# Routing attention and a hard-swish feed-forward: the first division a double step sooner, and two short settings instead of three behind each indexed transfer

## The chip, the core and the metric

The kernel runs on one core of a Trainium2 chip. The core has five engines, each with an instruction stream of its own: TensorE (PE in the profile; its weight loads are PEld), VectorE (DVE), ScalarE (ACT), GpSimd (POOL) and SyncE (SP). SyncE issues most of the transfers; ScalarE issues some, and GpSimd issues the indexed ones. Each engine takes its instructions in the order in which the kernel wrote them, and waits on semaphores where it needs another engine's result or a transfer's landing.

The metric is the device time of one execution in microseconds. The kernel before takes 937.38 us (median of three runs, from 936.87 to 940.17).

## What is computed

Attention with routing: queries and keys are assigned to the nearest of 16 centroids of their head, and a query sees only keys of its own cluster. The output, with the heads put side by side, goes through a feed-forward block with the hard-swish gate.

```python
B, H, S, D = 4, 8, 768, 64                       # 16 centroids per head
q_assign = argmax(q_n @ c_n, -1); k_assign = argmax(k_n @ c_n, -1)
scores = where(q_assign[:, None] == k_assign[None, :], q @ k.T / sqrt(D), -1e9)
attn = softmax(scores)
x = (attn @ v).transpose(0, 2, 1, 3).reshape(B * S, H * D)      # 3072 x 512
h = x @ w_in                                     # 512 x 2048
g = h * clip(h + 3, 0, 6) / 6
out = g @ w_out                                  # 2048 x 512
```

The matrices w_in and w_out arrive as 64-bit floats and are turned into 32-bit floats on the chip, by integer operations on their two halves.

## The kernel before

**Pairs of heads.** The 32 heads go through in 16 pairs, two heads to 128 partitions. Four pairs make up one batch (NKT = 4). The first eight pairs (batches 0 and 1) are done in full: all 768 x 768 scores of a head are computed, a mask made from the cluster assignment is added by a second matmul, and ScalarE takes the exponentials. The last eight pairs (batches 2 and 3) are sorted by cluster, so that only bands of the score matrix are needed.

**The early part** is a loop over double steps (`for n in range(0, ..., 2)`, L1399). One pair takes twelve steps (six double steps): two halves of the queries (hf) by six blocks of keys (j). A double step does the scores (L407) and exponentials (L430) of steps n and n + 1, adds the exponentials up on GpSimd (L437, L440) for the sums of the softmax, and multiplies the exponentials of the two steps before with the values (L450). In between stand the preparation of the next pair (transposes L325, cluster scores L344, `route` L351 to L378, `route_turn` L380 to L391), the loads of the q, k and v of coming pairs (in the double step with r == 6, by `load`, L209), and a handful of steps that decode the weights (`decoding_steps`, L224 to L270). One chunk of the weights takes five such steps, and its first also issues the load of the chunk two further on (L222, tile `raw`).

**Sums and division.** When both halves of a pair have been added up, `sum_up` (L467) lets TensorE add over the partitions (pd, L476), ScalarE copies the result (dn, L480), and SyncE stores it in device memory (sums, L483). The attention output without division (num, L459) is stored as xd by a transfer that stands in a list (L461). After the last pair of a batch `load_sums` (L487) reads all the sums of the batch back in another layout (plain, L489), `invert` takes their reciprocal on VectorE (L492) and stores it (rd, L493), and `complete` appends the three blocks of 256 tokens of the batch to `waiting` and calls `load_block` (L550). That one loads a block of xd (xb, L556) and the reciprocals for it, spread over the partitions (rb, L560). `divide` (L507) then multiplies xb by rb on VectorE (L510), in place. The feed-forward matmuls read xb.

**The order of these stages** is made by two lists. Whatever is put into `later` in one double step moves to `checks` at the end of that double step, and is executed at the end of the next one, by `check_all` (L1362). In batch 0 each stage puts the next into `later`, so that read-back, reciprocal, block load and division stand one double step apart. In batch 0 the sums of the last pair (pair 3) are stored in the double step n = 50, the read-back is issued at the end of n = 52, the reciprocal at the end of n = 54 (behind the `route` of the next pair), the block load at the end of n = 56 and the division at the end of n = 58. The first feed-forward matmuls (ph, L634) come in the double step n = 60, the first entry of `up_at` (L1343). In batch 1 the read-back is put out the same way, in the last double steps of the loop, while its `invert` and `complete` have fixed places in the late part (points 2 and 4, L1445).

**The late part** (L1443) is a plan of points. Each point issues what `late_plan` lists for the late pairs and then one item of the feed-forward of the batches that are ready. One pair starts every 28 points (SLOT). The feed-forward works on blocks of 256 tokens as 2 x 2 blocks with seven products instead of eight; for each of its units it loads sums of weight blocks (tx, L573, issued by ScalarE) from device memory.

**Indexed transfers.** For each late pair GpSimd scatters the rows of q (`scatter` with a = 0: qd, L1094) and of k and v together (a = 1: kvd, L1094) to their ranks, twelve transfers each (two heads by six columns of 128 rows), and later gathers the rows of the output back (`gather`: xn, L1109), twelve more. Behind each of these 36 transfers per pair stands `pause()`, which issues PAUSE settings of the one-column tile w_low (L1086). They write the value that is in it already.

Of the kernel before, what the change touches and what calls it, by code (L numbers as in the profile page):

```python
# [122 lines left out]
def fast_path(ctx, tc, ok, q, k, v, centroids, moe_w_in, moe_w_out, out):  # L123
# [57 lines left out]
    later = []  # L181

    def scratch(shape, name, dtype=F32):

        if st["early"]:
            return psum_m.tile(shape, dtype, name=name, tag="m")
        return psum_t.tile(shape, dtype, name=name, tag="t")
# [279 lines left out]
    def sum_up(g):  # L467
        b, kt = divmod(g, NKT)
        if kt == 0:
            for name in ("sums", "rd"):  # L470
                st[name, b] = dram.tile([NKT, 2, S], F32, name=f"{name}{b}")
        pd = scratch([P, 512], "pd")[:, 0:HALF]
        for t in range(2):
            for hf in range(2):
                r = (2 * t + hf) * 2 * C
                nc.tensor.matmul(  # L476
                    pd[r : r + 2 * C], lhsT=ones[:, 0 : 2 * C], rhs=st["acc", g, hf][:, t], start=True, stop=True
                )
        dn = nump.tile([P, HALF], F32, name="dn")
        nc.scalar.copy(out=dn, in_=pd)  # L480
        for hf in range(2):
            st.pop(("acc", g, hf))
        nc.sync.dma_start(st["sums", b][kt].rearrange("t (hf c) -> (t hf) c", hf=2), dn[0 : P : 2 * C])  # L483
        if kt == NKT - 1:
            later.append(lambda: load_sums(b))

    def load_sums(b):  # L487
        tok = plain[:, b]
        nc.sync.dma_start(tok, st["sums", b].rearrange("k t s -> (k t s)").rearrange("(p n) -> p n", p=P))  # L489

        def invert():
            nc.vector.reciprocal(out=tok, in_=tok)  # L492
            nc.sync.dma_start(st["rd", b].rearrange("k t s -> (k t s)").rearrange("(p n) -> p n", p=P), tok)  # L493
            return complete

        def complete():
            waiting.extend((b, m) for m in range(NHC))
            load_block()
            if b == 0:
                later.append(lambda: divide(0, 0))  # L500

        if b == 0:
            later.append(lambda: later.append(invert()))
        else:
            st["invert"], st["complete"] = invert, complete

    def divide(b, m):  # L507
        if ("rb", b, m) in st:
            xb, rb = st["xb", b, m], st.pop(("rb", b, m))
            nc.vector.tensor_tensor(out=xb, in0=xb, in1=rb, op=ALU.mult)  # L510
# [39 lines left out]
    def load_block():  # L550
        if waiting and st["free"]:
            b, m = waiting.pop(0)
            st["free"] = False
            xb = st["xb", b, m] = xbp.tile([P, NKT, 2 * P], F32, name="xb")
            part = slice(2 * m * P, 2 * (m + 1) * P)
            nc.sync.dma_start(xb, st["xd", b][:, :, part])  # L556
            if ("rd", b) in st:
                rb = st["rb", b, m] = xbp.tile([P, NKT, 2 * P], F32, name="rb", tag="xs")
                for t in range(2):
                    nc.sync.dma_start(  # L560
                        rb[t * D : (t + 1) * D], st["rd", b][:, t, part].unsqueeze(0).to_broadcast([D, NKT, 2 * P])
                    )
# [516 lines left out]
            op0=ALU.min, op1=ALU.max,  # L1079
        )  # L1080

    PAUSE = 3

    def pause():
        for _ in range(PAUSE):
            nc.gpsimd.memset(w_low, W_LOW)  # L1086
# [287 lines left out]
    with tc.manual_schedule():  # L1374
# [24 lines left out]
        for n in range(0, total + lag_d + 2, 2):  # L1399
# [11 lines left out]
            if m >= 0 and m % per_pair == per_pair - 1:  # L1411
                sum_up(m // per_pair)
                ready(m)
# [355 lines left out]
@with_exitstack  # L1769
def kernel(  # L1770
    ctx: ExitStack,
    tc: tile.TileContext,
    q: bass.AP,
    k: bass.AP,
    v: bass.AP,
    centroids: bass.AP,
    moe_w_in: bass.AP,
    moe_w_out: bass.AP,
    out: bass.AP,
):  # L1780
    ins = (q, k, v, centroids, moe_w_in, moe_w_out)
    flagp = ctx.enter_context(tc.tile_pool(name="flagp", bufs=1))
    ok = flagp.tile([1, 1], I32, name="ok")
    with ExitStack() as inner:
        good = fast_path(inner, tc, ok, *ins, out)
    with tc.If(good == 0):
        with ExitStack() as inner:
            general_path(inner, tc, *ins, out)
# [32 lines left out]
```

## Time and profile before

| | |
|---|---|
| median of three runs | 937.38 us (936.87 to 940.17) |
| the profiled execution | 940.63 us, of which the span of the program's instructions is 938.7 us |
| TensorE busy | 920.1 us (98%) |
| GpSimd busy | 586.9 us (63%), 1313 instructions |
| VectorE busy | 552.8 us (59%) |
| ScalarE busy | 334.7 us (36%) |
| transfers | 124.77 MB, 133 GB/s on average |

In a row of the timeline stand the start and the length in us, the engine (with a q where its sequencer issues a transfer), the line of the kernel, the operation, what it writes and reads, how many such instructions are merged in the row, and in brackets how long the engine idled before and what ended that. In a row of the groups stand, after the bar, the busy time in us, the mean of one in ns, and after the second bar the idle time before them with its causes. In a row of the waits stand the waiting engine, line and tile, what was waited for, the total in us, how often, and the longest. In a row of the windows stand the stretch, its length, then the busy time and number of instructions of PE, PEld, DVE, ACT and POOL, the granted clock of TensorE, the share of the transfer engines, and GB/s. In the chain stand start, length and what held the chain.

### The profile page before, as it was taken

The numbers are of one execution on the slowest core, as the hardware profiler recorded it, in microseconds if no ns is written. First come the engines' busy times: TensorE is split into PE (matmuls) and PEld (weight loads), VectorE is DVE, ScalarE is ACT, GpSimd is POOL, SyncE is SP. The second block draws the span as 40 slices with busy tenths as digits, with TensorE's granted clock in tenths as the row PEclk, the third lists the DMA queues.
The fourth block names the chain that finished last, engine by engine and source line by source line (L and its number), as shares of the span: only waits on it lengthen the run. The fifth ranks groups of instructions, "written<-read, shape, count | busy, mean of one in ns | idle before, by whom it ended". The sixth has DMA issues, their size and how long they took to land.

```text
span 938.7 us, 17537 instructions
## 1 busy us (share of the span) xinstructions
PE 920.1 (98%) x6350; PEld 721.7 (77%) x6350; DVE 552.8 (59%) x1299; ACT 334.7 (36%) x667; POOL 586.9 (63%) x1313
## 2 busy tenths in 40 slices
PE   8999989999999999999999999999999999999997
PEld 5444445555898898797897978888888899999996
DVE  6667647778876385384483573563571555536261
ACT  6888767765012332222232241241322311212020
POOL 3877876779376787878778777777887060303030
PEclk9999999999999999999999999999999999999999
DMA  8444565450465566474772835645563334323120
GB/s 199 137 134 128 160 181 141 140 166 34 119 196 164 140 173 154 131 208 93 197 199 80 218 101 155 167 146 131 132 175 96 87 84 120 100 73 108 57 68 27
DMA packets 177024, 124.77 MB, mean 133 GB/s; under 512 B 135681, under 2 KB 155169, under 8 KB 176929
## 3 DMA queue, kind: packets, MB, share of 16 engines
q1 hardware_dynamic: 153968, 76.52, 31.1%
q10 hardware_dynamic: 13744, 34.44, 12.5%
q0 software_dynamic: 9216, 12.60, 4.4%
q8 instruction: 52, 0.85, 0.4%
q14 instruction: 44, 0.35, 0.1%
HBM read 95.11 MB, written 28.41 MB: 132 GB/s over the span
## 4 chain that ended last, share of the span: by engine, by line
PE 91%; DVE 3%; ACT 2%; DMA 2%; issue 1%; SPq 0%; DVEq 0%; ACTq 0%
PE Y L725 18%; PE uY L686 16%; PE X L725 13%; PE uX L686 12%; PE ps L407 7%; PE pv L450 6%; PE ph L634 3%; PE pv L1196 3%; PE ps L978 2%; PE ps L1139 2%; PE pcs L344 1%; PE pv L1139 1%; PE pqk L325 1%; DMA rb<-rd 1%; PE pd L476 1%
## 5 line engine op out<-in xcount | busy, mean ns | idle before, releaser
L440 POOL TENSOR_TENSOR acc<-acc,ex 128x768 f32<-128x768 f32 x64 | 124.8, 1950 | 29.9 <-ACT ex L430 26.5
L1094 POOL DMA_INDIRECT qd<-qn,pos x96 | 98.7, 1028 | 45.7 <-DVE tx L576 17.9
L1109 POOL DMA_INDIRECT xn<-xsd,pos x96 | 92.3, 961 | 49.5 <-ACT sx L517 27.9
L676 POOL TENSOR_TENSOR g_sb<-g_sb 128x256 f32<-128x256 f32 x52 | 39.2, 776 | 121.7 <-DVE g_sb L520 120.6
L517 ACT ACTIVATE sx<-g_sb,half_c 128x512 f32<-128x512 f32 x88 | 63.6, 723 | 144.1 <-DVE g_sb L697 111.4
L1086 POOL MEMSET w_low<- 128x1 f32 x864 | 91.6, 106 | 33.4
L1094 POOL DMA_INDIRECT kvd<-kvn,pos x96 | 97.3, 1013 | 21.7 <-issue 21.7
L732 DVE TENSOR_TENSOR y<-y,Y 128x256 f32<-128x256 f32 x47 | 19.8, 421 | 128.4 <-PE Y L725 100.1
L686 PE MATMUL uX<-xb,w_in_sb 128*128 128x128 f32 x704 | 93.0, 275 | 0.0
L725 PE MATMUL X<-w_out_sb,g_sb 128*128 128x256 f32 x384 | 90.3, 382 | 0.0
L725 PE MATMUL Y<-T,g_sb 128*128 128x256 f32 x384 | 88.0, 381 | 0.0
L725 PE MATMUL Y<-w_out_sb,g_sb 128*128 128x256 f32 x384 | 87.7, 380 | 0.0
L686 PEld LDWEIGHTS uX<-xb,w_in_sb 128*128 128x128 f32 x704 | 85.7, 192 | 0.0
L725 PEld LDWEIGHTS Y<-T,g_sb 128*128 128x128 f32 x384 | 72.1, 190 | 13.0 <-issue 3.3
L725 PEld LDWEIGHTS X<-w_out_sb,g_sb 128*128 128x128 f32 x384 | 71.0, 190 | 13.8 <-issue 4.0
L725 PEld LDWEIGHTS Y<-w_out_sb,g_sb 128*128 128x128 f32 x384 | 71.8, 190 | 10.5 <-issue 1.0
L697 DVE TENSOR_TENSOR sx<-uX,sx 128x128 f32<-128x128 f32 x176 | 51.1, 291 | 48.3 <-ACT sx L704 35.9
L407 PE MATMUL ps<-xf 64*128 64x384 f32 x384 | 78.6, 487 | 0.3 <-ACT ex L430 0.3
L430 ACT ACTIVATE ex<-ps 128x768 f32<-128x768 f32 x96 | 73.0, 804 | 5.9 <-PE ps L407 5.8
L450 PE MATMUL pv<-ex,vt 128*64 128x384 f32 x384 | 72.5, 499 | 0.0
L697 DVE TENSOR_TENSOR g_sb<-uY,sx 128x128 f32<-128x128 f32 (+1 forms) x176 | 65.6, 414 | 0.0
L520 DVE SCALAR_TENSOR_TENSOR g_sb<-sx,g_sb 128x512 f32<-128x512 f32 x88 | 64.0, 730 | 1.5 <-ACT sx L517 1.3
(211 smaller groups left out, 1727.1 us busy)
## 6 DMA issues: line engine op xcount, KB each, us to landing
tx<-td ACTq DMA_DIRECT2D x86, 384.0 KB
raw<-in_moe_w_in_dram SPq DMA_DIRECT2D x16, 512.0 KB
raw<-in_moe_w_out_dram SPq DMA_DIRECT2D x16, 512.0 KB
xb<-xd SPq DMA_DIRECT2D x12, 512.0 KB
out_dram<-y SPq DMA_DIRECT2D x44, 128.0 KB
qk<-in_k_dram SPq DMA_DIRECT2D x16, 192.0 KB
vt<-in_v_dram SPq DMA_DIRECT2D x16, 192.0 KB
xd<-num SPq DMA_DIRECT2D x16, 192.0 KB
```

The lines of the kernel that those rows point to most:

```text
L407: nc.tensor.matmul(st["ps", n][:, t, 0:HALF], lhsT=x[r, NCH + j], rhs=x[r, hf * NHC : (hf + 1) * NHC], start=first, stop=last, skip_group_ ...
L430: nc.scalar.activation(out=ex, in_=sc, func=ACT.Exp, scale=SM_SCALE)
L440: nc.gpsimd.tensor_tensor(out=acc, in0=acc, in1=ex, op=ALU.add)
L450: nc.tensor.matmul(pv[t * D : (t + 1) * D], lhsT=vt[:, t, j], rhs=ex[:, t], start=(j == 0), stop=(j == NCH - 1),)
L517: nc.scalar.activation(out=r, in_=h, func=ACT.Relu, bias=half_c, scale=1.0 / 6.0)
L520: nc.vector.scalar_tensor_tensor(out=g, in0=r, scalar=1.0, in1=h, op0=ALU.min, op1=ALU.mult)
L686: nc.tensor.matmul(dst, lhsT=w[:, kt], rhs=x(kt), start=(kt == 0), stop=(kt == HK - 1))
L697: nc.vector.tensor_tensor(out=out_, in0=in0, in1=in1, op=ALU.add)
L725: nc.tensor.matmul(bank[:, half * HC : (half + 1) * HC], lhsT=g_sb[:, kind, i], rhs=w[:, i], start=(first and i == 0), stop=(last and i == ...
L1086: nc.gpsimd.memset(w_low, W_LOW)
L1094: i = nc.gpsimd.indirect_dma_start(out=rows[name, g, t], in_=src[:, j, t].rearrange("p a d -> p (a d)") if a else src[:, j, t], in_offset= ...
L1109: nc.gpsimd.indirect_dma_start(out=xn[:, j, t], out_offset=None, in_=rows["xsd", g, t], in_offset=bass.IndirectOffsetOnAxis(ap=pos[:, 0, j ...
```

## The change

`load_sums` is called at once in `sum_up`, directly behind the store of the last sums, instead of being put into `later`. In batch 0 the read-back is thus issued in the double step n = 50, and the three stages that follow from it come one double step sooner too: the reciprocal at the end of n = 52, the block load at the end of n = 54, the division at the end of n = 56. In batch 1 the read-back comes one double step sooner; the stages behind it keep their places. And `pause()` issues two settings instead of three.

```diff
@@ sum_up @@
         nc.sync.dma_start(st["sums", b][kt].rearrange("t (hf c) -> (t hf) c", hf=2), dn[0 : P : 2 * C])
         if kt == NKT - 1:
-            later.append(lambda: load_sums(b))
+            load_sums(b)
@@ before pause @@
-    PAUSE = 3
+    PAUSE = 2
```

## The prediction

> **What bounds the kernel now.** I read the page first: busy shares, the 40 slices, the granted clock, the chain. They show whose time the span is.
>
> ```profile
> span 938.7 us, 17537 instructions
> PE 920.1 (98%) x6350; PEld 721.7 (77%) x6350; DVE 552.8 (59%) x1299; ACT 334.7 (36%) x667; POOL 586.9 (63%) x1313
> PE   8999989999999999999999999999999999999997
> PEclk9999999999999999999999999999999999999999
> PE 91%; DVE 3%; ACT 2%; DMA 2%; issue 1%; SPq 0%; DVEq 0%; ACTq 0%
> ```
>
> TensorE is busy 920.1 of 938.7 us and holds 91% of the chain. So the order of work on the other engines can only be worth what TensorE idles: 18.6 us in all, some at both ends. One slice stands out, the sixth (117 to 141 us), with 8 where its neighbours have 9. I therefore asked for the stretches around it, for TensorE's order of time there, and for the long stretch in which GpSimd runs its indexed transfers.
>
> ```profile
> core 0: us, PE busy (x) PEld busy (x) DVE busy (x) ACT busy (x) POOL busy (x), PEclk, DMA share, GB/s
> ...
> 133.30:136.80 3.50, 0.05 (x1) 0.03 (x1) 1.30 (x1) 0.67 (x2) 3.42 (x3) 1.00 0.22 59
> ...
> 138.00:141.30 3.30, 3.30 (x9) 2.68 (x8) 0.00 (x0) 0.00 (x0) 0.05 (x1) 0.50 0.72 237
> ...
> 300.00:726.00 426.00, 422.46 (x3046) 360.16 (x3044) 233.01 (x651) 117.10 (x222) 331.17 (x1008) 1.00 0.55 148
> ```
>
> ```profile
> 132.70 0.65 PE L325 MATMUL pqk<-ident,qk 128*128 128x128 f32 x4
> 136.80 5.38 PE L634 MATMUL ph<-xb,w_in_sb 128*128 128x256 f32 x16 [3.45 <-DVE xb L510]
> 142.02 0.60 PE L325 MATMUL pqk<-ident,qk 128*128 128x128 f32 x4
> ...
> 151.02 3.72 PE L634 MATMUL ph<-xb,w_in_sb 128*128 128x256 f32 x16
> 154.68 0.34 PE L407 MATMUL ps<-xm 64*128 64x384 bf16 x2
> ```
>
> The reader sees one hole: TensorE ends its transposes at 133.35 (132.70 + 0.65) and starts the first feed-forward matmuls at 136.80, after 3.45 us of waiting for the first division (DVE, xb, L510). The granted clock is then 0.50 between 138.0 and 141.3. The same sixteen matmuls take 142.02 - 136.80 = 5.22 us to the next instruction here and 154.68 - 151.02 = 3.66 us the next time, so the half clock costs 1.56 us more. **The hole costs 3.45 + 1.56 = 5.0 us**, 0.53% of the median. [...]
>
> From 300 to 726 us TensorE idles 426.00 - 422.46 = 3.5 us in all: that is what is left to win where GpSimd's transfers run.
>
> **What holds the division back.** The chain, in that window, and then VectorE and the queue of SyncE:
>
> ```profile
> 126.55 8.68 DMA rb<-rd
> ```
>
> ```profile
> 113.02 0.69 DVE L255 TENSOR_SCALAR wunit<-wtop 128x512 uint32<-128x512 uint32 x1
> 121.28 0.56 DVE L358 TENSOR_REDUCE mx<-pr 128x24 f32<-128x384 f32 x1 [7.56 <-PE pr L355]
> 123.41 0.44 DVE L492 RECIPROCAL plain<-plain 128x48 f32<-128x48 f32 x1
> 127.67 0.69 DVE L266 TENSOR_TENSOR w_out_sb<-wtop,wunit 128x512 f32<-128x512 f32 x1
> 130.57 0.69 DVE L261 SCALAR_TENSOR_TENSOR wunit<-raw,wunit 128x512 f32<-128x512 uint32 x1
> 135.36 1.30 DVE L510 TENSOR_TENSOR xb<-xb,rb 128x1024 f32<-128x1024 f32 x1 [4.09 <-DMA rb<-rd]
> ```
>
> ```profile
> 113.64 0.56 SPq L483 DMA_DIRECT2D sums<-dn  x1
> 114.25 0.43 SPq L461 DMA_DIRECT2D xd<-num  x1
> 114.77 0.38 SPq L222 DMA_DIRECT2D raw<-in_moe_w_out_dram  x1
> 115.38 0.33 SPq L489 DMA_DIRECT2D plain<-sums  x1
> 115.80 1.26 SPq L209 DMA_DIRECT2D qk<-in_q_dram  x2
> 117.11 2.01 SPq L209 DMA_DIRECT2D qk<-in_k_dram  x2
> 119.16 1.11 SPq L209 DMA_DIRECT2D vt<-in_v_dram  x2
> 123.88 0.33 SPq L493 DMA_DIRECT2D rd<-plain  x1
> 124.30 0.38 SPq L222 DMA_DIRECT2D raw<-in_moe_w_out_dram  x1
> 125.83 1.37 SPq L560 DMA_DIRECT2D rb<-rd  x2
> ```
>
> The sums are stored at 113.64 and read back at 115.38. Their reciprocal runs only at 123.41, because in its present place it stands behind the reduction of the routing scores, which waits 7.56 us for TensorE's transposes (pr). The store of the reciprocals (rd) follows at 123.88, the broadcast load (rb) at 125.83, and that lands 8.68 us after its second issue.
>
> **The change, part by part.**
>
> *The first division, batch 0.* The read-back is now issued in the step that stores the sums, so the reciprocal, the block load and the division each come one double step sooner in the orders written out.
>
> The read-back itself gains almost nothing: it must wait for the landing of the sums. In the trace it went out at 115.38, when SyncE had just come free; the landing lies between 114.2 (end of the issue) and 115.38. I take the late end, since no landing that these rows bound is shorter. What it is moved past on SyncE: the store of num (114.25) and one weight load (114.77) now stand behind it, up to 1.1 us later (115.38 - 114.25). The weight load is for a chunk two ahead, and num is needed only by the block load near 123; neither has a reader within that time.
>
> The reciprocal gains most. It now stands before the 7.56 us wait: VectorE is idle from 113.71 (113.02 + 0.69). Its operand lands some 2.0 us after the issue: the rd store of the same tile, issued at 123.88, had landed when the rb load went out at 125.83, so at most 1.95. So: reciprocal at 115.4 + 2.0 = 117.4, done 117.8, rd out at about 117.9 instead of 123.88.
>
> SyncE serves in order, so the six loads of q, k and v (115.80 to 120.27, 4.5 us) now wait behind rd and run from 118.3 to 122.8, 2.5 us late. Their q and k are read at TensorE's transposes of 132.70, ten us on: covered. The block load comes next, and the rb pair 0.6 us behind it: first rb at 123.4 instead of 125.83. **That is 2.4 us sooner, where the reciprocal gains 6, because the group of loads is now in between.** With the same 8.68 us for the transfer rb lands at 135.23 - 2.4 = 132.8; the division ends 1.43 us later (wake-up and 1.30) at 134.3, and TensorE starts at 134.4 instead of 136.80. **Remaining hole: 134.4 - 133.35 = 1.0 us; hole removed: 2.4 us.** Bounds: if rb is served faster since no weight load goes out ahead of it, the hole is gone (3.45); if the q, k and v transfers directly ahead slow it by 2.4 us, nothing is won.
>
> With 1.0 us of idling I expect no half clock, worth 1.56; the bounds are 0 and 1.56, and I take the whole because the short TensorE waits of this trace elsewhere show full clock (the 426 us stretch with its idling has 1.00).
>
> What waits behind the division on VectorE: five decode steps (127.67 to 131.26 in the trace) now stand behind it and would end near 134.3 + 3.6 = 137.9. Their readers are the weights of the second matrix and the raw buffers, both used two chunks later; the next VectorE work that TensorE needs, the clip behind the sixteen matmuls, comes after 134.4 + 3.66 = 138.1. Covered, with 0.2 us to spare and the activation on ScalarE in between; if the cover goes, the cost is the overlap.
>
> *The same edit for batch 1.*
>
> ```profile
> 238.06 0.44 SPq L461 DMA_DIRECT2D xd<-num  x1
> 240.74 0.32 SPq L489 DMA_DIRECT2D plain<-sums  x1
> ```
>
> Here the read-back waited until 240.74, so it goes out no sooner; num moves from 238.06 to about 241.1, 3 us later. It is read by the block loads of batch 1, after three blocks of batch 0: nothing. Bounds: 0 to the 0.4 us that the issues behind it shift.
>
> *Two settings instead of three.*
>
> ```profile
> L1094 POOL DMA_INDIRECT qd<-qn,pos x96 | 98.7, 1028 | 45.7 <-DVE tx L576 17.9 <-issue 14.8 <-DVE pos L1077 8.7
> L1086 POOL MEMSET w_low<- 128x1 f32 x864 | 91.6, 106 | 33.4
> ```
>
> 864 settings are three behind each of 288 transfers. One setting is 106 ns and 33.4 / 864 = 39 ns of idling before it, so 288 x 145 ns = 42 us of GpSimd go: 5.2 us per pair of heads (36 transfers). GpSimd was busy 331.17 of the 426 us above and nearly all its idle time there lies between these short instructions. But who waits for it? TensorE's waits from 300 to 726 us, by length:
>
> ```profile
> PE ps L978 <- ACT xsort L979: 1.4, 1, 1.4
> PE rk L1048 <- DVE steps L1012: 0.8, 1, 0.8
> ...
> PE uX L686 <- DMA tx<-td: 0.3, 1, 0.3
> ```
>
> None is for GpSimd or for a gathered or scattered row. So 42 us of an engine off the chain are worth 0; bounds: 3.5 us won (all the idling), and on the other side what the rival below prices.
>
> **Sum.** 2.4 (hole) + 1.56 (clock) + 0 + 0 = 4.0 us. The profiled execution took 940.63 us, 1.9 outside its span of 938.7; it would become 936.6. It lies 3.25 us above the median of 937.38. From the median: 933.4 us, 0.43% faster. What separates this kernel from no change is about 0.5%, 4.7 us, so the forecast sits just inside it. The two bounds of the first edit give 932.4 (all 5.0 us) and 937.4.
>
> **The rivals.**
>
> *The transfer comes no sooner.* The six loads stand directly ahead of rb, and if they delay its landing by 2.4 us or more the hole stays. For it: 8.68 us is long beside the at most 1.95 of the rd store, so rb may be queued for most of it. Against: the weight load of 124.30, which used to stand ahead, now stands behind. Time: 937.4.
>
> *The half clock is not in the ordinary executions.* The four known times go from 936.87 to 940.63; a difference of 3.8 us is more than twice 1.56. If a hole of 3.45 us halves the clock in some executions only, the median holds none of it, and 2.4 us is all: 935.0. For it: the profiled execution is the slowest of the four. Against: nothing else in the trace tells the executions apart. [...]
>
> *GpSimd sets the pace after all.* It is nearly gapless from 300 to 726, and a wait put down to ScalarE or VectorE may start from its rows. Then up to 3.5 us more: 933.4 - 3.5 = 929.9. Against: the waits above name other work.
>
> *Closer transfers delay the tx loads (slower).*
>
> ```profile
> q0 software_dynamic: 9216, 12.60, 4.4%
> tx<-td ACTq DMA_DIRECT2D x86, 384.0 KB
> ```
>
> Every half-size block unit on TensorE needs a 384 KB load. The indexed transfers come about 10% closer together, and each could push back a tx load. To end above 942.1 (0.5% slower) 4.7 + 4.0 = 8.7 us are needed, 0.10 us for each of the 86 loads; at 0.15 the time is 946.3. For it: one tx wait of 0.3 us is there already, so some loads arrive just in time. Against: these transfers are 4.4% of the engines' time. [...]
>
> **How the numbers follow.** Forecast (hole shrinks by 2.4 to 3.45, clock stays up) 0.52; transfer no sooner 0.13; no half clock 0.16; GpSimd's pace 0.11; tx loads 0.08. Faster by over 0.5% means under 932.7: GpSimd's 0.11, and half of the forecast's case, that with hardly any hole left (0.26): 0.37. Slower: 0.08. The rest, 0.55, lies between. The range reaches from between GpSimd's case and the forecast, 930.9, to just above no gain, 937.8; outside lie the tx case and half of GpSimd's.
>
> **What would show it.** The changed trace should have the reciprocal at about 117.4, ahead of the 7.56 us wait; rd before the q loads; the first rb near 123.4; a TensorE wait at the first ph of 0 to 1.1 us, with the clock at 1.00 behind it; 576 settings and GpSimd's busy time down by some 31 us (288 x 106 ns); TensorE's idling from 300 to 726 within 1 us of 3.5. The forecast is wrong if ph still waits over 2 us, if a new VectorE wait stands at the clip near 139, or if tx appears among TensorE's waits with more than 2 us.

## The result, and the profile after

The changed kernel took 1020.07 us (median of six runs, 997.46 to 1032.58), against 939.19 us (936.87 to 942.15) for the kernel before beside it, 8.6% more by these medians. The ratio of the fast runs, 1.0679 with a 95% interval of 1.0617 to 1.0742, sets only the two fastest of its six runs (997.46 and 1008.49) against the kernel before, since the other four lie over 1.5% above the fastest. It is slower by 6.8% at the least, and the prediction of 933.4 us was wrong in size and in sign.

The page of the changed kernel (its profiled run is the fastest of the six, 997.46 us), the lines that answer to those shown of before:

```profile
span 995.6 us, 17246 instructions
PE 949.1 (95%) x6350; PEld 735.7 (74%) x6350; DVE 552.9 (56%) x1299; ACT 334.4 (34%) x667; POOL 557.4 (56%) x1025
PE   8999999999979899999999899989989999999997
PEclk9999999999989979999999999989999999999999
q8 instruction: 52, 0.85, 0.4%
L1086 POOL MEMSET w_low<- 128x1 f32 x576 | 61.9, 108 | 16.7
```

The 288 settings are gone (576 instead of 864). TensorE is busy 949.1 us with the same 6350 matmuls, and the eights and sevens in its row, some with a lower granted clock below them, now stand in the middle of the span, where GpSimd runs its indexed transfers. The sixth slice, of which the prediction spoke, is mended.

*The first division.* VectorE and the queue of SyncE around it, then TensorE, in order of time:

```profile
117.16 0.45 DVE L492 RECIPROCAL plain<-plain 128x48 f32<-128x48 f32 x1 [3.34 <-DMA plain<-sums]
121.36 0.56 DVE L358 TENSOR_REDUCE mx<-pr 128x24 f32<-128x384 f32 x1 [3.76 <-PE pr L355]
131.41 2.33 DVE L510 TENSOR_TENSOR xb<-xb,rb 128x1024 f32<-128x1024 f32 x1 [3.71 <-DMA rb<-rd]
```

```profile
115.42 0.33 SPq L489 DMA_DIRECT2D plain<-sums  x1
115.81 0.42 SPq L461 DMA_DIRECT2D xd<-num  x1
...
117.64 0.32 SPq L493 DMA_DIRECT2D rd<-plain  x1
118.05 1.26 SPq L209 DMA_DIRECT2D qk<-in_q_dram  x2
...
123.26 1.29 SPq L560 DMA_DIRECT2D rb<-rd  x2
```

```profile
132.78 0.65 PE L325 MATMUL pqk<-ident,qk 128*128 128x128 f32 x4
133.89 3.69 PE L634 MATMUL ph<-xb,w_in_sb 128*128 128x256 f32 x16 [0.45 <-DVE xb L510]
137.42 0.60 PE L325 MATMUL pqk<-ident,qk 128*128 128x128 f32 x4
```

The wait at the first feed-forward matmuls is 0.45 us where it was 3.45, and the sixteen of them take 137.42 - 133.89 = 3.53 us to the next instruction where they took 5.22.

*The long stretch with the indexed transfers.* Busy time of the engines in three windows of the changed kernel (the clock and the DMA share stand behind the five engines), and then what TensorE waited for from 300 to 726 us (total, times, longest):

```profile
138.00:141.30 3.30, 3.30 (x25) 1.41 (x28) 2.86 (x5) 3.27 (x8) 0.27 (x2) 1.00 0.74 247
350.20:360.20 10.00, 8.91 (x38) 6.96 (x39) 6.74 (x17) 2.35 (x5) 3.15 (x9) 0.50 0.31 90
...
300.00:726.00 426.00, 402.48 (x2767) 334.45 (x2765) 209.88 (x594) 105.05 (x200) 274.79 (x677) 0.98 0.51 136
```

```profile
PE uY L686 <- issue: 5.3, 10, 0.8
PE uX L686 <- issue: 3.4, 8, 0.5
PE pv L1196 <- issue: 2.2, 5, 0.8
```

Here TensorE idles 426.00 - 402.48 = 23.5 us instead of 3.5, and the three rows that lead its waits, 10.9 us, are put down to "issue": it waited for nothing that the profile shows, neither data nor a semaphore. In the kernel before, one stall of 0.5 us from 245 us on is put down to "issue"; here 43 are, 21.5 us in all. What that looks like, engine by engine, in order of time: TensorE, and below it GpSimd in the same microseconds.

```profile
266.38 0.78 PE L686 MATMUL uY<-xs,w_in_sb 128*128 128x128 f32 x3
267.63 0.35 PE L686 MATMUL uY<-xs,w_in_sb 128*128 128x128 f32 x1 [0.47 <-issue]
267.82 0.39 PE L686 MATMUL uX<-xs,tx 128*128 128x128 f32 x2
269.01 0.39 PE L686 MATMUL uX<-xs,tx 128*128 128x128 f32 x2 [0.81 <-issue]
269.24 0.78 PE L686 MATMUL uX<-xb,w_in_sb 128*128 128x128 f32 x3
270.47 0.36 PE L686 MATMUL uX<-xb,w_in_sb 128*128 128x128 f32 x1 [0.46 <-issue]
```

```profile
267.21 0.96 POOL L1094 DMA_INDIRECT qd<-qn,pos  x1 [0.16 <-issue]
268.17 0.27 POOL L1086 MEMSET w_low<- 128x1 f32 x2
268.60 0.96 POOL L1094 DMA_INDIRECT qd<-qn,pos  x1 [0.16 <-issue]
```

In these microseconds TensorE gets a handful of matmuls per indexed transfer, stops, and goes on, in the rhythm of GpSimd: GpSimd's transfers start every 268.60 - 267.21 = 1.39 us, TensorE resumes at 267.63, 269.01 and 270.47. In the packet records the last packets of the transfer before end at 267.61, 268.99 and 270.37, just ahead of each. It is not so clear everywhere: of the 43 stalls 14 end within 0.15 us behind the last packet of an indexed transfer, where moments drawn at random within 0.7 us of their ends do so in one case of ten. Most of the stalled time, 16.6 of the 21.5 us, stands at L686, whose matmuls have 128 columns; L1196, with 112 to 352 columns, has 2.2. Behind a row of stalls the clock goes down too, as the window from 350.20 shows. With three settings, in the kernel before, the transfers of a row start 298.24 - 296.70 = 1.54 us apart:

```profile
296.70 0.96 POOL L1094 DMA_INDIRECT kvd<-kvn,pos  x1 [0.15 <-issue]
297.65 0.43 POOL L1086 MEMSET w_low<- 128x1 f32 x3
298.24 0.96 POOL L1094 DMA_INDIRECT kvd<-kvn,pos  x1 [0.15 <-issue]
```

### The profile page after: what moved, and what is told of

The parts are those of the page before. It is cut to its first block, busy times and chain, and to the rows that moved or that the text cites. A ratio compares the mean times of both kernels' runs of the same rounds, so it can differ in the third digit from the quotient of the medians.

```text
span 995.6 us, 17246 instructions
## 1 busy us (share of the span) xinstructions
PE 949.1 (95%) x6350; PEld 735.7 (74%) x6350; DVE 552.9 (56%) x1299; ACT 334.4 (34%) x667; POOL 557.4 (56%) x1025
## 5 line engine op out<-in xcount | busy, mean ns | idle before, releaser
L1109 POOL DMA_INDIRECT xn<-xsd,pos x96 | 94.6, 986 | 101.7 <-DMA xsd<-xr 41.2
L686 PE MATMUL uX<-xb,w_in_sb 128*128 128x128 f32 x704 | 99.3, 279 | 7.4 <-issue 5.8
L686 PEld LDWEIGHTS uX<-xb,w_in_sb 128*128 128x128 f32 x704 | 88.4, 194 | 10.8 <-issue 10.7
L725 PE MATMUL X<-w_out_sb,g_sb 128*128 128x256 f32 x384 | 91.1, 383 | 1.5 <-DVE g_sb L520 1.3
L725 PE MATMUL Y<-T,g_sb 128*128 128x256 f32 x384 | 88.0, 381 | 0.0
L725 PE MATMUL Y<-w_out_sb,g_sb 128*128 128x256 f32 x384 | 87.7, 380 | 0.0
L725 PEld LDWEIGHTS X<-w_out_sb,g_sb 128*128 128x128 f32 x384 | 70.7, 190 | 16.4 <-issue 4.4
L725 PEld LDWEIGHTS Y<-T,g_sb 128*128 128x128 f32 x384 | 72.1, 190 | 13.0 <-issue 3.4
L725 PEld LDWEIGHTS Y<-w_out_sb,g_sb 128*128 128x128 f32 x384 | 71.8, 190 | 10.5 <-issue 1.0
L1086 POOL MEMSET w_low<- 128x1 f32 x576 | 61.9, 108 | 16.7
L697 DVE TENSOR_TENSOR sx<-uY,sx 128x128 f32<-128x128 f32 x88 | 25.4, 288 | 76.2 <-PE uY L686 35.2
```

The lines of the kernel that those rows point to most:

```text
L686: nc.tensor.matmul(dst, lhsT=w[:, kt], rhs=x(kt), start=(kt == 0), stop=(kt == HK - 1))
L697: nc.vector.tensor_tensor(out=out_, in0=in0, in1=in1, op=ALU.add)
L725: nc.tensor.matmul(bank[:, half * HC : (half + 1) * HC], lhsT=g_sb[:, kind, i], rhs=w[:, i], start=(first and i == 0), stop=(last and i == ...
L1109: nc.gpsimd.indirect_dma_start(out=xn[:, j, t], out_offset=None, in_=rows["xsd", g, t], in_offset=bass.IndirectOffsetOnAxis(ap=pos[:, 0, j ...
```

## The experiments

The theory to begin with: transfers that start 1.39 us apart instead of 1.54 take from TensorE the supply of its instructions (theory A, the spacing). The rival: the shift of the whole late part by some 5 us, which the first edit brings, puts GpSimd's work under other work of TensorE (theory B, the phase).

Each group of experiments ran on one chip, together with the kernel before. This turned out to matter, so the chips have letters here: A for the first group, B, C and D for the next three, E for the last two. On which chip the result above was measured is not known.

### First group, chip A: the two edits apart, and other numbers of settings

All are the kernel before with the first edit (but for the second of them) and a value of PAUSE:

```diff
-            later.append(lambda: load_sums(b))
+            load_sums(b)        # not in "two settings only"
...
-    PAUSE = 3
+    PAUSE = 3                   # sums only; 2: two settings only; 1 and 4: the other two
```

> The first division a double step sooner, with three settings behind each indexed transfer as before. Theory A (the closer spacing of the indexed transfers, 1.39 us from start to start instead of 1.54, robs TensorE): only the hole at the first division changes, so 4 to 5 us less than before, about 934 us, and TensorE idles about 4 us between 245 and 750 us. Theory B (the late part was shifted by 5 us against something else, and the spacing has nothing to do with it): as slow as the changed kernel, some 1000 us or more.

> Two settings instead of three, the division where it was. Theory A: all of the loss, 1000 to 1040 us, with TensorE idling over 25 us between 245 and 760 us and the clock at 0.50 in several stretches. Theory B: within 5 us of before, 935 to 945 us.

> The division sooner, and one setting behind each transfer (start to start about 1.23 us). Theory A: worse than with two, over 1040 us, since TensorE gets still less between the transfers. Theory B: no order in it, anything from 934 to 1030 us.

> The division sooner, and four settings (start to start about 1.70 us, so 36 transfers of a pair of heads take some 61 us, about a pair's whole stretch on TensorE of 59.6 us). Theory A: no loss to collisions, 932 to 936 us, unless GpSimd is now late for TensorE, which would show as TensorE waits that lead back to gathered rows. Theory B: no order, 934 to 1030 us.

| chip A; kernel before 940.88 us | median, us | ratio to before | 95% interval |
|---|---|---|---|
| first edit alone, three settings | 934.77 | 0.9935 | 0.9907 to 0.9964 |
| two settings alone | 1024.78 | 1.0914 | 1.0820 to 1.1009 |
| first edit, one setting | 1172.51 | 1.2457 | 1.2346 to 1.2568 |
| first edit, four settings | 964.31 | 1.0243 | 1.0195 to 1.0291 |

One of the eleven executions of the kernel before on this chip took 1339.56 us at a mean granted clock of 0.655, where the other ten took 937.13 to 945.85; what happened in it isn't known.

The whole loss belongs to the two settings, and without the first edit it is as large (1024.78 - 940.88 = 84 us here, 81 in the result above): theory B falls. One setting costs nearly three times as much; TensorE's busy time from 300 to 726 us, and its longest waits there, which have the same name with longer times:

```profile
300.00:726.00 426.00, 328.52 (x2091) 267.19 (x2091) 168.87 (x475) 82.77 (x157) 184.69 (x336) 0.84 0.38 103
```

```profile
PE uY L686 <- issue: 27.7, 33, 2.4
...
PE pv L1196 <- issue: 9.6, 8, 3.7
```

Four settings are slower than three as well, but for a cause that has a semaphore: GpSimd comes late with its rows. TensorE's waits there, from 245 to 800 us:

```profile
PE ps L978 <- DMA piece<-kvd: 12.9, 3, 7.1
```

### Second group, chip B: spacing against number, pair against row, bytes

```diff
 # one wide: one setting as long as three
-        for _ in range(PAUSE):
-            nc.gpsimd.memset(w_low, W_LOW)
+        nc.gpsimd.memset(st["long"], 0.0)        # 128x368 bf16
 # alternate: by the column j
-        for _ in range(PAUSE):
+        for _ in range(2 if j % 2 else 4):
 # keys only: two behind scatters of k and v, three elsewhere
-                pause()
+                pause(2 if a else 3)
 # wide q, one setting: scatter the q rows of both heads (left out here: qd is made
 # twice as wide, and the load of its rows picks the head's half)
-... in_=src[:, j, t].rearrange("p a d -> p (a d)") if a else src[:, j, t],
+... in_=(src[:, j, t] if a else src[:, j]).rearrange("p a d -> p (a d)"),
```

> The first division stands a double step sooner, and behind each indexed transfer stands one wide setting (128x368 bf16, about 0.40 us by the 0.417 us of the 128x384 one) in place of three narrow ones, so that the transfers should start about 1.54 us apart, as with three. Theory of the spacing (TensorE runs short when transfers start closer than about 1.5 us, whatever stands between them): the loss stays away, 932 to 938 us, TensorE idle under 3 us from 245 to 750. Rival, the number of short instructions between two transfers counts (each lets something else through): one is fewer than two, so the time is above 1020 us.

> The first division a double step sooner; four settings behind the transfers of even columns and two behind those of odd columns, so that the mean spacing is that of three settings, and every second transfer comes as close as with two. If each close pair costs by itself, about half of the loss of two settings comes back: 970 to 985 us. If only the mean rate over several transfers counts (something with a store of its own is drained), 933 to 938 us.

> The first division a double step sooner; two settings only behind the scatters of keys and values (64 KB each, 96 of the 288 transfers, half of the bytes), three elsewhere. If every close transfer costs alike, a third of the 85 us: about 963 us. If the cost goes with the bytes, half or more: 975 to 990 us. If scatters of q and gathers carry it, below 940 us.

> The first division a double step sooner, one setting behind each transfer, and the scatter of q moves the rows of both heads (64 KB in place of 32 KB, as many rows; half of what is moved is not read). Compared with one setting and the narrow q (1172.5 us, where TensorE lost some 5 us beneath a run of q scatters and some 15 us beneath a run of those of keys and values). If bytes are what makes a transfer cost TensorE time, the runs of q lose some 15 us too: about 1250 us. If rows or transfers count, or what TensorE does beneath them, 1160 to 1190 us.

| chip B; kernel before 937.46 us | median, us | ratio to before | 95% interval |
|---|---|---|---|
| one wide setting | 933.05 | 0.9950 | 0.9934 to 0.9967 |
| four and two by turns | 932.04 | 0.9941 | 0.9925 to 0.9958 |
| two behind keys and values | 932.01 | 0.9941 | 0.9925 to 0.9958 |
| one setting, wide rows of q | 932.68 | 0.9949 | 0.9929 to 0.9969 |

The last line fits no theory: with one setting, and with more bytes than the kernel that took 1172.51 us, nothing is lost. Either wide rows and mixed numbers cure the loss, or the chip decides. None of the four can then be read as it was meant.

### Third group, chip C: the same kernels on another chip

No new edit: the changed kernel, the one with one setting (e3), and the one with wide rows (e8), side by side.

> The changed kernel as it stands, beside the next two in one call, on one chip. The loss of two settings and of one was seen in kernels that ran on one chip (the changed kernel itself, two settings alone, one setting); the four kernels after them, with as close or closer transfers and no loss, ran on another. If the chip or what surrounds it decides, the three kernels of this call share a fate: all three at 930 to 935 us, or the changed kernel at 1000 to 1035 us and both with one setting above 1100 us. If the kernel decides (three settings behind some transfers, or wider rows of q, cure it), the changed kernel is at 1000 to 1035 us, one setting with narrow rows above 1100 us, and one setting with wide rows of q at 932 us.

> One setting, narrow rows of q, the first division sooner. If the chip decides: 930 to 936 us where the changed kernel beside it is at 930 to 935 us, above 1100 us where that is above 1000 us. If the kernel decides: 1150 to 1180 us whatever the chip.

> One setting, wide rows of q, the first division sooner; it took 932.7 us before. If the chip decides: with the changed kernel beside it, 932 us or above 1100 us. If the kernel decides: 932 us whatever the chip.

On chip C, beside 937.25 us for the kernel before, the changed kernel took 932.15 us (ratio 0.9945, 0.9923 to 0.9967), one setting 932.60 us (0.9952, 0.9932 to 0.9973) and wide rows 931.97 us (0.9946, 0.9927 to 0.9964). The kernel with one setting is the one that took 1172.51 us on chip A. So the chip decides, or what surrounds the program on it.

The profile of the changed kernel on chip C, the page, then the same window as above, then the same microseconds of TensorE's timeline:

```profile
span 930.2 us, 17246 instructions
PE 918.1 (99%) x6350; PEld 721.2 (78%) x6350; DVE 554.1 (60%) x1299; ACT 334.4 (36%) x667; POOL 557.5 (60%) x1025
```

```profile
300.00:726.00 426.00, 425.18 (x3095) 362.26 (x3094) 234.96 (x655) 120.65 (x230) 305.99 (x756) 1.00 0.56 149
```

```profile
266.37 0.61 PE L686 MATMUL uX<-xs,tx 128*128 128x128 f32 x4
266.81 1.06 PE L686 MATMUL uX<-xb,w_in_sb 128*128 128x128 f32 x8
267.70 0.61 PE L686 MATMUL uY<-xs,tx 128*128 128x128 f32 x4
```

The matmuls of L686 that stalled stand here without a gap, and TensorE idles 0.8 us of the 426. Between the two executions of one kernel lie 995.6 - 930.2 = 65.4 us: TensorE idles 46.5 us (995.6 - 949.1) instead of 12.1, which is 34.4, and is busy 31.0 us longer. The mean granted clock of 0.983 against 0.999 accounts for about 16 of these by estimate (995.6 x 0.017 = 16.9 us lost, against 930.2 x 0.001 = 0.9); the other 15 lie inside the busy rows and stay unexplained. The weight loads, which overlap with them (949.1 + 735.7 us of busy time in a span of 995.6), are longer by 735.7 - 721.2 = 14.5 us in all.

It is not GpSimd that behaves otherwise. Its rows with one setting, on chip A (first) and on chip C, in the same microseconds:

```profile
277.56 0.96 POOL L1094 DMA_INDIRECT kvd<-kvn,pos  x1 [0.19 <-issue]
278.52 0.11 POOL L1086 MEMSET w_low<- 128x1 f32 x1
278.82 0.96 POOL L1094 DMA_INDIRECT kvd<-kvn,pos  x1 [0.19 <-issue]
```

```profile
277.73 0.96 POOL L1094 DMA_INDIRECT kvd<-kvn,pos  x1 [0.19 <-issue]
278.68 0.12 POOL L1086 MEMSET w_low<- 128x1 f32 x1
278.99 0.95 POOL L1094 DMA_INDIRECT kvd<-kvn,pos  x1 [0.19 <-issue]
```

The same durations and the same 1.26 us from start to start; only TensorE's instructions stay out on the one and not on the other.

### Fourth group, chip D

No new edit: the changed kernel, one setting (e3) and one wide setting (e5).

> The changed kernel as it stands, on whatever chip this call gets. If the loss belongs to few chips: 930 to 934 us, the kernel before at 936 to 939 us with little scatter. If it belongs to most and the two chips without it were the exception: 1000 to 1035 us, the kernel before scattering from 937 to 946 us as in the first group.

> One setting, the first division sooner. It shares the fate of the changed kernel beside it: 932 to 934 us where that is below 935 us, above 1100 us where that is above 1000 us. A time in between, 940 to 1000 us, would say that the chips differ by degrees.

> One wide setting of 0.40 us in place of three narrow ones, the first division sooner. Where the changed kernel beside it loses: 932 to 940 us if the spacing of the transfers (1.54 us as with three) is what counts, above 1020 us if the number of instructions between them is. Where the changed kernel does not lose: 932 to 935 us by either.

Beside 937.60 us for the kernel before, the changed kernel took 932.14 us (0.9945, 0.9929 to 0.9962), one setting 932.86 us (0.9952, 0.9936 to 0.9968), one wide setting 933.13 us (0.9958, 0.9941 to 0.9975). Chip D is like B and C. With no loss there, the wide setting says nothing on spacing or number.

### Fifth and sixth group, chip E: the loss comes back

No new edit: the changed kernel, the first edit alone (e1) and four and two by turns (e6); then, somewhat later on the same chip, one wide setting (e5).

> The changed kernel as it stands, on whatever chip this call gets: 931 to 933 us on a chip like the last three, 1000 to 1035 us on one like the first.

> Only the first division sooner, three settings kept. On a chip without the loss: if the settings are worth nothing there, the same as the changed kernel beside it, 931.5 to 933 us; if fewer settings win some of TensorE's idling, 933 to 936 us. On a chip with the loss: 932 to 939 us, as in the first group.

> Four settings and two by turns, the first division sooner. On a chip without the loss: 931.5 to 932.5 us, as before. On a chip with it: 970 to 985 us if each close pair costs by itself, 933 to 940 us if only a row of close transfers does.

> One wide setting of 0.40 us in place of three narrow ones, the first division sooner. On a chip with the loss (the kernel before at 937 to 949 us): 932 to 942 us if the spacing of the transfers counts, above 1020 us if the number of instructions between them does. On a chip without it (the kernel before at 936 to 939 us): 932 to 935 us by either, and the question stays open.

| chip E | median, us | kernel before, us | ratio | 95% interval |
|---|---|---|---|---|
| the changed kernel | 1068.90 | 945.39 | 1.1345 | 1.1270 to 1.1420 |
| first edit alone, three settings | 938.67 | 945.39 | 0.9930 | 0.9908 to 0.9952 |
| four and two by turns | 939.75 | 945.39 | 0.9956 | 0.9929 to 0.9984 |
| one wide setting | 943.16 | 948.61 | 0.9954 | 0.9926 to 0.9981 |

TensorE's busy time from 300 to 726 us in these four kernels, in the order of the table, one fence each:

```profile
300.00:726.00 426.00, 377.32 (x2459) 308.47 (x2458) 191.41 (x541) 94.50 (x180) 235.29 (x585) 0.93 0.45 119
```

```profile
300.00:726.00 426.00, 422.95 (x3062) 360.39 (x3061) 233.45 (x650) 118.85 (x226) 330.86 (x1008) 1.00 0.55 148
```

```profile
300.00:726.00 426.00, 420.46 (x3039) 357.23 (x3038) 232.37 (x649) 117.72 (x225) 327.67 (x1008) 1.00 0.55 148
```

```profile
300.00:726.00 426.00, 419.74 (x3010) 356.53 (x3008) 234.83 (x646) 116.05 (x220) 360.00 (x504) 0.99 0.59 147
```

With two settings throughout TensorE idles 48.7 us here (426.00 - 377.32); with three 3.1, by turns 5.5, with one wide one 6.3. Two things follow for this chip. (The wide setting ran in the later group, without the changed kernel beside it; that the loss was still there is taken from the chip, and from its kernel before, which was at 948.61 us.) First, one instruction between two transfers does nearly as well as three, if it is as long: the time from transfer to transfer counts, not how many instructions stand there. The rows of the kernel with the wide setting show that time, 281.30 - 279.75 = 1.55 us:

```profile
279.75 0.97 POOL L1092 DMA_INDIRECT kvd<-kvn,pos  x1 [0.17 <-issue]
280.72 0.42 POOL L1084 MEMSET long<- 128x368 bf16 x1
281.30 0.97 POOL L1092 DMA_INDIRECT kvd<-kvn,pos  x1 [0.17 <-issue]
```

Second, by turns every other transfer follows as closely as in the changed kernel (281.27 - 279.88 = 1.39 us, the one before it 279.88 - 278.19 = 1.69), and nearly nothing is lost: a single close pair does no harm here (5.5 us of idling), a row of twelve does (48.7). That is the second case of its expectation, in which the mean rate over several transfers counts; no run shows that anything is drained.

What differs between A and E on the one side and B, C and D on the other is not settled. The kernel before is itself slower where the loss is (940.88, 945.39 and 948.61 us against 937.25 to 937.60), so a little of it may be there with three settings. Whether it is the chip, the place that the program gets in memory, or other work on the chip can't be told from one core's records. Nor was it tried what it is that TensorE lacks. One thing can be set aside as far as the trace shows it. The row q8 of the page above, of the kind "instruction", has 52 packets with 0.85 MB. Whose they are the page doesn't say; the author takes them for TensorE's, one to each 244 of its 12700 matmuls and weight loads. In the changed kernel only 3.8 of the 32.0 us of TensorE's stalls from 245 us on (all idling over 0.2 us, whatever it is put down to) lie within half a microsecond of such a packet, so late packets of q8 can explain no more than these. The other 28.2 us lie away from them, and the wait called "issue" is left without a cause.

## Why the prediction was wrong

**The step that failed** is the price of the settings: "So 42 us of an engine off the chain are worth 0; bounds: 3.5 us won (all the idling), and on the other side what the rival below prices." On the chips B, C and D nothing speaks against it: there two settings (932.14 and 932.15 us), two behind keys only (932.01) and four and two by turns (932.04) are the same, and 932.15 us lies in the predicted range; three settings throughout, with the first edit, weren't run there. The third setting is worth 84 us on A (1024.78 - 940.88) and 130 us on E (1068.90 - 938.67), because it keeps the indexed transfers 1.54 us apart; the result above is of their sort, with 1020.07 - 939.19 = 81 us lost. The step asked who waits for GpSimd, found nobody, and set the lower bound by the one thing through which transfers and TensorE were seen to meet, the tx loads. What the settings bought was no wait in any row: the trace of before has a single stall of 0.5 us without a visible cause in the late part, for with three settings there are hardly any. How TensorE comes to stall when the transfers are closer stays open. (A small misreading beside it: of GpSimd's 94.8 us of idling from 300 to 726, not nearly all lies between the short instructions; 15.2 us are waits for VectorE and ScalarE.)

**The rival with the right sign had the wrong mechanism.** "Closer transfers delay the tx loads" (0.08) asked for 0.10 us for each of the 86 loads. In the changed kernel one tx wait of 1.4 us stands among the waits; the idling is put down to "issue". How the indexed transfers and the tx loads share the transfer engines, on which that rival turns, was tested by no run. TensorE's stalls aren't put down to a transfer, and the packets of the indexed transfers are no slower where the loss is: from 250 to 800 us their median is 56 ns in the changed kernel above and 56 ns on chip C. Nor could the trace shown have said on which chip a run would fall; a chance for the sign could only have come from asking what the transfers do to TensorE when they come closer, not who waits for them.

**Step by step, the rest:**
- The reciprocal: predicted at 117.4, ahead of the routing reduction; it came at 117.16. Right, and so is the cause: its operand's transfer is what it now waits for. rd: 117.9 predicted, 117.64 measured. First rb: 123.4 predicted, 123.26 measured, held back by the q, k and v loads as said.
- The hole: 1.0 us was to remain, 0.45 did. That this is near is partly luck, for two sizes were off and largely cancelled: rb landed about 1.5 us sooner than the 132.8 predicted (the division starts at 131.41, 0.13 us behind it if that wake-up is as before), and the division took 2.33 us instead of 1.30. Why it takes longer there was not tried.
- The half clock at 138 is gone: 1.00 in that window; 1.56 us were predicted, and 5.22 - 3.53 = 1.69 measured. The second rival, in which it isn't there in most executions, found no support. The mean granted clock of every execution was measured: on B, C and D it is 0.995 to 0.998 in the 22 of the kernel before (0.997 in the profiled one, with its 3.4 us at half clock) and 0.998 to 0.999 in the seven of the changed kernel. So all but one of the 22 lose as much of the clock as the profiled one, or more.
- The first rival falls: the transfer came sooner. The first edit alone is faster by 0.65% and 0.70% (A, E), 6.1 and 6.7 us, more than the 0.43% forecast. In its profile on chip A, TensorE idles only 0.7 us from 300 to 726 where before it idled 3.5:

```profile
300.00:726.00 426.00, 425.28 (x3094) 362.30 (x3093) 235.48 (x655) 120.67 (x230) 333.75 (x1008) 1.00 0.56 149
```

- So between these two executions the short waits of the late part go as well, 2.8 us, a term that the sum doesn't have: 3.0 (hole) + 1.7 (clock) + 2.8 = 7.5 us, of the 8.3 by which the spans differ (938.7 and, for the first edit alone, 930.4). Whether the first edit removes them isn't shown. The same kernel idles 3.1 us there on chip E, and the kernel before was profiled on a chip that isn't known, in the slowest of the four executions known then. On chip C the medians differ by 937.25 - 932.15 = 5.1 us, of which hole and clock make 4.7.
- The third rival, GpSimd setting the pace, falls: on chip C one setting (932.60) wins nothing over two (932.15).
- The decode steps behind the division cost nothing, as predicted: behind the first sixteen matmuls TensorE goes straight on at 137.42. Nor did the edit for batch 1: on chip C all that TensorE waits for from 142 to 255 us is 0.6 us, for masks of the scores.
- Of the signs named beforehand, "TensorE's idling from 300 to 726 within 1 us of 3.5" is the one that caught it: 23.5 us. None of the three signs that were to say that the forecast is wrong came: ph waits 0.45 us, TensorE is busy without a gap from 138.0 to 141.3, and tx has 1.4 us.

In the trace of the changed kernel the granted clock is at 0.50 for 3.413, 6.827 and 10.24 us at a time, in six places from 245 to 800 us. No long idle stretch came ahead of them: no wait of TensorE from 245 us on is longer than 1.6 us, and in the 3.41 us ahead of each of the six drops it was busy for 1.43 to 2.15 us. So the rows of short stalls were paid for twice here: with the idling itself, 23.5 us from 300 to 726, and with the lower clock behind it, by the estimate above about 16 us of the whole span.

## What to carry to other kernels

An engine that nobody waits for can still be worth its pauses: the time between its transfers is spacing that another engine may live on (on chip E TensorE idled 3.1 us of the 426 with three settings and 48.7 with two), and no wait in the profile of the version that has it names it. So an edit that only removes idle work is tried alone, on more than one chip, and with the spacing varied in both directions; here, on chip A, three settings stand between two cliffs, the loss below (1024.78 us with two alone) and GpSimd's lateness above (964.31 us with four). The version to keep is the first edit with three settings: it is faster than the kernel before on both chips that have the loss (0.9935 and 0.9930). Where there is no loss it wasn't run; the changed kernel stands at 0.9945 there.

## What the runs showed of the hardware

- Indexed transfers of GpSimd in rows of twelve, 1.39 us from start to start, left TensorE idle, mostly in waits for nothing visible, on some chips: 23.5, 35.4 (two settings alone, chip A) and 48.7 us of 426. At 1.26 us, with one setting, it was 97.5 (426.00 less the 328.52 busy). At a mean spacing of about 1.55 us, evenly or by turns, it was 0.7 to 6.3.
- The kernels with two settings and with one idled 0.8 to 0.9 us there on three other chips, with rows of the same length on GpSimd. One kernel, one setting: 1172.51, 932.60 and 932.86 us on three chips. A verdict from one chip, on a change of this sort, is a verdict on that chip.
- The stalls aren't spread evenly. In the waits of the changed kernel from 245 us on, "issue" has 16.6 us at L686 (128 columns) and 0.2 at L725 (256 columns); on chip E, to 800 us, 34.4 at L686 and 2.3 at Y of L725, and with one setting 75.4 and 4.0. The number of columns isn't the whole of it: with one setting 24.5 us stand at L1139, whose matmuls have 240 and 352.
- The granted clock fell to 0.50 behind 3.41 us in which TensorE was busy for 1.43 to 2.15 us, in six places of one trace, with no stall over 1.6 us.
